# Token parts of 256 and 320 columns in layer 1, and 256-column halves in layer 2's second product

## The chip, the core and the metric

The kernel runs on one core of one Trainium2 chip. The metric is the device time of one execution in microseconds. The kernel before takes 853.9 us, the median of three runs (852.61 to 855.0).

## What is computed

The reference is a packed attention followed by two feed-forward layers, all in float32.

```python
# q, k, v: (4, 8, 576, 64); p: (4, 8, 32, 64)
p_packed = softmax(p @ k.T / 8) @ v          # 32 packed rows per head
x = softmax(q @ p_packed.T / 8) @ p_packed   # as (2304 tokens, 512)
h = x @ w1_in;  g = max(0.01 * h, h);  x = g @ w1_out      # 512 -> 2048 -> 512
h = x @ w2_in;  g = h * tanh(softplus(h));  out = g @ w2_out
```

2304 tokens are 4 batches of 576. The weights arrive as 64-bit floats and are converted on the chip.

## The kernel before, in words

Every large product is made of three matmuls on operands in the float32r type: each operand is split into a rounded part (index 0, "hi") and the rest (index 1, "lo"), and `PASSES` lists hi x hi, hi x lo, lo x hi. The first index picks the stationary operand (the weights that are loaded into the array), the second the moving one (whose columns stream through). So two of three passes in a row have the same stationary operand. Each such `mm` call gives one weight load (LDWEIGHTS) and one matmul in the trace; an `mm` on plain float32 operands gives two of each. The warm-up `warm` (L604 to L607) is of the second kind: 16 calls of 128 x 128 by 128 columns, called four times at the start, 128 matmuls in the trace.

Layer 1's first product (`l1_h`, L372 to L394) is folded with the attention: `packed_w` (L354 to L370) multiplies the packed values with `w1_in`, and `l1_h` multiplies the result `pw` (stationary, 128 x 128) with the attention weights `a2` (moving) of one batch. One call makes 128 of the 2048 hidden features for one half of a batch, `HALF` = 288 tokens, in 6 matmuls (2 head groups x 3 passes) into one PSUM bank `ps_h1` (tag "h", 2 buffers). ScalarE applies the leaky ReLU twice, rounded into `gx[:, 0]` and in full into `gf` (L391, L392), and VectorE writes the difference into `gx[:, 1]` (L393). `gf` has 3 buffers, `gx` 4; the tag "gx" is lent to attention tiles early on (`spare`, L199).

`l1_y` (L403 to L428) multiplies `w1_out` (stationary, four blocks `e` of 128 output features) with `gx` (moving, 288 columns): 12 matmuls that add into four banks `ps_y` (tag "y", 4 buffers, so all four belong to one part of the tokens at a time). At the last feature of a part the banks are evicted into `yp` blocks of `TB` = 384 tokens; a part that crosses a block's edge is evicted in two pieces (L422 copy on ScalarE, L424 add on VectorE). In the second pass `y_parts` splits finished blocks into `yh` and `yl` (L437, L439).

The order of this work is the list `slots` (L338 to L346): pass, batch, half `hb`, feature `f`; 128 slots, each one `l1_h` and, three slots later (`LAG`), one `l1_y`. Between the matmuls `tick` issues background steps (attention of later batches, `packed_w`, weight conversion) by a fixed plan, the string `SCHED`: a plan by counted ticks, not by time. The main loop waits, while the program is built, until the attention weights of the slot's half are there (L655). The whole program is issued in this written order; every engine runs its instructions in order.

Layer 2 goes through 96 steps of one feature block of 128 for one block of 384 tokens. `l2_h` (L444 to L455): 12 matmuls of 384 columns, `w2_in` stationary, `yh`/`yl` moving. `l2_g` (L457): two Mish activations and a subtraction. `l2_o` (L468 to L488), two steps later: the tokens are now the stationary operand (`gx`, three groups of 128) and `w2_out` the moving one, all 512 columns at once: 9 matmuls into three banks `ps_o`, evicted after each fourth step. The PE order is thus 12 matmuls of 384, 9 of 512, 12 of 384, and so on.

Of the kernel before, what the change touches and what calls it, by code (L numbers as in the profile page):

```python
# [8 lines left out]
F32 = mybir.dt.float32  # L9
F32R = mybir.dt.float32r  # L10
# [19 lines left out]
def tile_packed_attention_moe2(ctx: ExitStack, tc: tile.TileContext, q, k, v, p, w1i, w1o, w2i, w2o, out):  # L30
    nc = tc.nc
    B, H, S, D = q.shape
# [3 lines left out]
    R = 6  # L36
    SP = S // R
    HALF = S // 2
    NG = H // 4
    NE = DM // 128  # L40
    TB = 384
# [4 lines left out]
    mm = nc.tensor.matmul  # L46
# [5 lines left out]
    ident = const.tile([128, 128], F32, name="ident")  # L52
    ppT = const.tile([128, B * NG, 2, 2 * NP], F32, name="ppT")

    prog = {"h": -1, "y": -1, "pw": -1, "yb": -1, "h2": -1, "o": -1, "cv": -1}
# [6 lines left out]
    wi, wo, w2a, w2b = {}, {}, {}, {}  # L62
# [89 lines left out]
    a2_t = {}  # L152
    packed, ready = set(), set()
# [4 lines left out]
    def load_wide(src, nm, u):  # L158
        b, g = divmod(u, NG)
        if nm == "k":  # L160
            t = pwp.tile([SP, 4, R, D], F32, tag="pw", name=f"st_{nm}")
        else:
            t = ylp.tile([SP, 4, R, D], F32, tag="yl", name=f"st_{nm}")
        nc.sync.dma_start(t.rearrange("p h r d -> p h (r d)"), src[b, 4 * g : 4 * g + 4].rearrange("h (p r) d -> p h (r d)", r=R))
        staged[nm, u] = t
# [16 lines left out]
    def load_v(u):  # L182
        if u >= B * NG:
            return
        b, g = divmod(u, NG)
        t = ylp.tile([SP, 4, R, D], F32, tag="yl", name="raw_v") if u == 1 else raw.tile([SP, 4, R, D], F32, tag="rawv", name="raw_v")
        nc.sync.dma_start(t.rearrange("p h r d -> p h (r d)"), v[b, 4 * g : 4 * g + 4].rearrange("h (p r) d -> p h (r d)", r=R))
        raws["v", u] = t

    def load(src, nm, u):  # L190
        if u >= B * NG:
            return
        b, g = divmod(u, NG)
        t = raw.tile([SP, R, 4, D], F32, tag="raw" + nm, name=f"raw_{nm}")
        for h in range(4):
            nc.sync.dma_start(t[:, :, h, :], src[b, 4 * g + h].rearrange("(p r) d -> p r d", r=R))
        raws[nm, u] = t.rearrange("p r h d -> p r (h d)")

    def spare(nm):  # L199

        return gp.tile([128, S], F32, tag="gx", name=nm, bufs=4)

    def transpose_in(t, o, bank):
        for hp in range(2):
            for hb in range(2):
                ps = bank()
                for r in range(3):
                    nc.tensor.transpose(ps[:, r * SP : (r + 1) * SP], t[:, 3 * hb + r, 128 * hp : 128 * hp + 128], ident[:SP, :SP])  # L208
                nc.scalar.copy(o[hp][:, hb * HALF : (hb + 1) * HALF], ps[:, :HALF])
                yield  # L210

    def pack(u, bank, first=False):
# [12 lines left out]
        for hb in range(2):  # L225
            ps = bank()
            for hp in range(2):
                mm(ps[64 * hp : 64 * hp + 64, :HALF], pT[:, 2 * u + hp, :], kT[hp][:, hb * HALF : (hb + 1) * HALF], start=True, stop=True)  # L228
            nc.vector.reduce_max(mx2[:, hb : hb + 1], ps[:, :HALF], axis=AX.X)
            sc.append(ps)  # L230
# [6 lines left out]
        for hb in range(2):  # L237
            nc.scalar.activation(
                e1[:, hb * HALF : (hb + 1) * HALF], sc[hb][:, :HALF], AF.Exp, bias=nmb, scale=c_s, accum_out=sm2[:, hb : hb + 1]
            )  # L240
# [40 lines left out]
    def spread(u, bank, first=False):  # L281
# [11 lines left out]
        for hb in range(2):  # L293
            ps = bank()
            for hp in range(2):
                mm(ps[64 * hp : 64 * hp + 64, :HALF], ppT[:, u, hp, :], qT[hp][:, hb * HALF : (hb + 1) * HALF], start=True, stop=True)  # L296
            nc.vector.transpose(out=bt[:, hb * HALF : (hb + 1) * HALF], in_=ps[:, :HALF])
            yield
# [41 lines left out]
    for pas in range(2):  # L340
        for b in range(B):
            n_g = 2 if b in SPLIT[pas] else 1
            for c in range(n_g):
                for hb in range(2):
                    w = 8 // n_g
# [26 lines left out]
    def l1_h(i):  # L372
        pas, b, hb, f = slots[i][:4]
        pw = pw_t[(pas * B + b) * 2 + f % 8 // 4]
        fc = f % 4 * 128
        ps = psh.tile([128, 512], F32, tag="h", name="ps_h1")[:, :HALF]
        n = 0
        for g in range(NG):
            for x, y in PASSES:
                mm(  # L380
                    ps,
                    pw[:, g, x, fc : fc + 128],
                    a2_t[b, g][:, y, hb * HALF : (hb + 1) * HALF],
                    start=n == 0,
                    stop=n == 3 * NG - 1,
                )
                n += 1
        prog["h"] = i
        gf = gp.tile([128, HALF], F32, tag="gf", name="gf", bufs=3)
        gx = gp.tile([128, 2, HALF], F32R, tag="gx", name="gx", bufs=4)  # L390
        nc.scalar.activation(gx[:, 0], ps, AF.Prelu, alpha=0.01)  # L391
        nc.scalar.activation(gf, ps, AF.Prelu, alpha=0.01)  # L392
        nc.vector.tensor_tensor(out=gx[:, 1], in0=gf, in1=gx[:, 0], op=ALU.subtract)  # L393
        return gx  # L394
# [3 lines left out]
    def block(d, pool, dt, k, tag, nm):  # L398
        if k not in d:
            d[k] = pool.tile([128, NE, TB], dt, tag=tag, name=f"{nm}{k}")  # L400
        return d[k]

    def l1_y(i, gx, tick):  # L403
        pas, b, hb, f, first, last, part, final = slots[i]
        if first:
            ystate["b"] = [psy.tile([128, 512], F32, tag="y", name="ps_y") for _ in range(NE)]
        yb = ystate["b"]

        pieces, c = [], 0
        while c < HALF:  # L410
            k, o = divmod(b * S + hb * HALF + c, TB)
            n = min(TB - o, HALF - c)
            pieces.append((k, c, o, n))
            c += n
        for e in range(NE):
            for n, (x, y) in enumerate(PASSES):
                mm(yb[e][:, :HALF], wo[f][:, x, e * 128 : (e + 1) * 128], gx[:, y], start=first and n == 0, stop=last and n == 2)  # L417
            if last:
                for k, c, o, n in pieces:
                    dst = block(ypart, ylp, F32, k, "yl", "yp")[:, e, o : o + n]  # L420
                    if pas == 0 and part == 0:
                        nc.scalar.copy(dst, yb[e][:, c : c + n])  # L422
                    else:
                        nc.vector.tensor_tensor(out=dst, in0=yb[e][:, c : c + n], in1=dst, op=ALU.add)  # L424
            tick()
        prog["y"] = i
        if last and final and pas == 1:
            spawn(y_parts(pieces))  # L428
# [39 lines left out]
    def l2_o(s, gx, tick):  # L468
        fq, blk, fi = s // (4 * NB2), s // 4 % NB2, s % 4
        if fi == 0:  # L470
            ostate["b"] = [pso.tile([128, 512], F32, tag="o", name="ps_o") for _ in range(3)]
        ob = ostate["b"]
        w = w2b[fq * 4 + fi]
        if fq == 0 and fi == 3:
            outp[blk] = op_.tile([128, 3, 512], F32, tag="op", name="op")
        for t in range(3):
            for n, (x, y) in enumerate(PASSES):
                mm(ob[t], gx[:, x, t * 128 : (t + 1) * 128], w[:, y], start=fi == 0 and n == 0, stop=fi == 3 and n == 2)  # L478
            if fi == 3:
                dst = outp[blk][:, t]  # L480
                if fq == 0:
                    nc.scalar.copy(dst, ob[t])
                else:
                    nc.vector.tensor_tensor(out=dst, in0=ob[t], in1=dst, op=ALU.add)  # L484
                if fq == 3:
                    store(dst, blk * TB + t * 128)
            tick()
        prog["o"] = s  # L488
# [45 lines left out]
    def wait_for(cond):  # L534
        n = 0
        while not cond():
            tick(True)
            n += 1
            assert n < 1000

    with tc.manual_schedule():

        with ExitStack() as st1:
            a2p = st1.enter_context(tc.tile_pool(name="a2p", bufs=1, side="right"))
            pwp = st1.enter_context(tc.tile_pool(name="pwp", bufs=2, side="right"))
            gp = st1.enter_context(tc.tile_pool(name="gp", bufs=3, side="right"))
            psa = st1.enter_context(tc.tile_pool(name="psa", bufs=2, space=PSUM))
            psh = st1.enter_context(tc.tile_pool(name="psh", bufs=2, space=PSUM))
# [38 lines left out]
            for n in range(3, 8):  # L587
                x = ((n - 3) // 2 * NB2 + NB2 - 1) * 4 + (n - 3) % 2 * 2 + 1
# [59 lines left out]
            for i, (pas, b, hb, f, *_) in enumerate(slots):  # L648
                if pas and st_att is not None:
                    wait_for(lambda: (B * NG - 1, 1) in ready)  # L650
                    st_att.close()
                    st_att = None
                    yp = ctx.enter_context(tc.tile_pool(name="yp", bufs=1, reuse_waits="tile"))
                kk = (pas * B + b) * 2 + f % 8 // 4
                wait_for(lambda: prog["pw"] >= kk and all((b * NG + g, hb) in ready for g in range(NG)))  # L655
                pend.append((i, l1_h(i)))
                tick()
                if len(pend) > LAG:
                    i0, gx = pend.pop(0)
                    wait_for(lambda: slots[i0][3] in wo)  # L660
                    l1_y(i0, gx, tick)
# [49 lines left out]
```

## Time and profile before

| | |
|---|---|
| median of three runs | 853.9 us |
| the profiled execution's own time | 853.85 us |
| its span (first to last instruction) | 852.0 us |
| granted TensorE clock, mean | 0.997 |
| DMA, mean over the span | 63 GB/s |

The trace shows one execution. PE is TensorE's matmuls, PEld its weight loads, which overlap the matmuls; DVE is VectorE, ACT ScalarE, POOL GpSimd. Durations in the groups of instructions are those of one instruction in the pipe; neighbouring matmuls overlap, so the interval between two is read from the chain of waits or from their starts, not from the mean duration.

### The profile page before, as it was taken

To read this page: it belongs to the slowest core of one execution; us is meant where nothing else is said; L and a number is where in the kernel's file an instruction comes from. 1 tells how busy PE (TensorE), PEld (TensorE's weight loads), DVE (VectorE), ACT (ScalarE), POOL (GpSimd) and SP (SyncE) were. 2 spreads that over 40 slices of the span, in tenths; PEclk is the share of its full clock that TensorE was granted. 3 is DMA by queue.
4 is the path that set the end of the run, shared out by engine and by line. 5 is a ranking of instruction groups with operands and counts; after the bars stand their busy time and mean duration, and the time that the engine had idled before them with its cause. 6 is when DMAs were issued, how large, how long until landed. Compare 5 with 4: busy or idle time off the path is not lost.

```text
span 852.0 us, 13012 instructions
## 1 busy us (share of the span) xinstructions
PE 832.2 (98%) x5344; PEld 745.4 (87%) x5344; DVE 369.3 (43%) x725; ACT 308.5 (36%) x781; POOL 131.2 (15%) x134
## 2 busy tenths in 40 slices
PE   8889999999999999999999999999999999999997
PEld 7777789788999989898999999999999999999996
DVE  2787643533756733237574111342234532432222
ACT  3555445454444433434444223322223322222221
POOL 1233201101102211113343000120001200110000
PEclk9999999999999999999999999999999999999999
DMA  9963333220332300002132000230002200102112
GB/s 221 310 160 81 105 71 71 56 57 1 100 100 99 99 1 1 2 1 70 40 115 75 1 1 1 75 98 25 1 25 82 83 9 1 50 1 75 38 37 75
DMA packets 52570, 53.52 MB, mean 63 GB/s; under 512 B 31264, under 2 KB 44064, under 8 KB 52512
## 3 DMA queue, kind: packets, MB, share of 16 engines
q1 hardware_dynamic: 52512, 52.70, 21.9%
q8 instruction: 42, 0.69, 0.3%
q14 instruction: 16, 0.13, 0.1%
HBM read 47.97 MB, written 4.72 MB: 62 GB/s over the span
## 4 chain that ended last, share of the span: by engine, by line
PE 91%; DVE 4%; DMA 2%; ACT 1%; issue 1%; SPq 0%; POOL 0%; ACTq 0%; DVEq 0%; POOLq 0%
PE ps_h L452 24%; PE ps_o L478 23%; PE ps_y L417 23%; PE ps_h L380 11%; PE ps_pw L364 3%; DMA st_q<-in_q_dram 2%; PE ps_a L265 2%; PE ps_a L208 1%; PE ps_a L296 1%; PE ps_a L228 1%; PE ps_a L256 0%; DVE cv L129 0%; DVE cv L127 0%; DVE cv L131 0%; DVE gx L393 0%
## 5 line engine op out<-in xcount | busy, mean ns | idle before, releaser
L417 PE MATMUL ps_y<-gx,wo 128*128 128x288 f32 x1536 | 240.0, 300 | 1.1 <-DVE yp L424 1.1
L417 PEld LDWEIGHTS ps_y<-gx,wo 128*128 128x128 f32 x1536 | 212.6, 189 | 23.5 <-issue 15.8
L478 PE MATMUL ps_o<-w2b,gx 128*128 128x512 f32 x864 | 216.7, 395 | 0.0
L452 PE MATMUL ps_h<-yh,w2a 128*128 128x384 f32 x768 | 210.7, 335 | 0.0
L478 PEld LDWEIGHTS ps_o<-w2b,gx 128*128 128x128 f32 x864 | 161.6, 188 | 31.1
L463 DVE TENSOR_TENSOR gx<-gf,gx 128x384 fp32r<-128x384 f32 x96 | 54.2, 565 | 269.2 <-ACT gf L462 269.2
L461 ACT ACTIVATE gx<-ps_h 128x384 fp32r<-128x384 f32 x96 | 47.1, 491 | 269.3 <-PE ps_h L452 269.3
L452 PEld LDWEIGHTS ps_h<-yh,w2a 128*128 128x128 f32 x768 | 140.8, 188 | 3.8
L393 DVE TENSOR_TENSOR gx<-gf,gx 128x288 fp32r<-128x288 f32 x128 | 69.7, 544 | 144.9 <-ACT gf L392 144.2
L452 PE MATMUL ps_h<-yl,w2a 128*128 128x384 f32 x384 | 129.0, 336 | 0.0
L380 PE MATMUL ps_h<-a,pw 128*128 128x288 f32 x768 | 125.0, 297 | 2.4 <-ACT pw L365 1.8
L380 PEld LDWEIGHTS ps_h<-a,pw 128*128 128x128 f32 x768 | 108.5, 188 | 8.5 <-issue 3.8
L391 ACT ACTIVATE gx<-ps_h 128x288 fp32r<-128x288 f32 x128 | 52.6, 411 | 129.2 <-PE ps_h L380 129.1
L452 PEld LDWEIGHTS ps_h<-yl,w2a 128*128 128x128 f32 x384 | 72.0, 188 | 3.9
L140 POOL TENSOR_TENSOR w2a<-cv,w2a 128x512 fp32r<-128x512 f32 x16 | 21.9, 1370 | 226.4 <-ACT w2a L139 226.4
L392 ACT ACTIVATE gf<-ps_h 128x288 f32<-128x288 f32 x128 | 52.2, 408 | 0.0
L462 ACT ACTIVATE gf<-ps_h 128x384 f32<-128x384 f32 x96 | 46.5, 484 | 0.0
L439 POOL TENSOR_TENSOR yl<-yp,yh 128x288 fp32r<-128x288 f32 (+2 forms) x48 | 31.9, 690 | 83.3 <-ACT yh L437 82.9
L129 DVE SCALAR_TENSOR_TENSOR cv<-st,cv 128x512 uint32<-128x512 uint32 x48 | 40.1, 835 | 1.1
L140 POOL TENSOR_TENSOR wo<-cv,wo 128x512 fp32r<-128x512 f32 x16 | 20.9, 1304 | 108.2 <-ACT wo L139 108.2
L484 DVE TENSOR_TENSOR op<-ps_o,op 128x512 f32<-128x512 f32 x54 | 34.5, 683 | 3.5 <-PE ps_o L478 3.5
L131 DVE SCALAR_TENSOR_TENSOR cv<-st,cv 128x512 uint32<-128x512 uint32 x48 | 34.5, 719 | 1.0
(109 smaller groups left out, 565.6 us busy)
## 6 DMA issues: line engine op xcount, KB each, us to landing
st<-in_moe_w_in_dram SPq DMA_DIRECT2D x32, 512.0 KB, 3.8
st<-in_moe_w_out_dram SPq DMA_DIRECT2D x32, 512.0 KB, 3.5
raw_v<-in_v_dram SPq DMA_DIRECT2D x8, 576.0 KB, 4.8
raw_k<-in_k_dram SPq DMA_DIRECT2D x24, 144.0 KB, 3.3
raw_q<-in_q_dram SPq DMA_DIRECT2D x24, 144.0 KB, 3.1
out_dram<-op SPq DMA_DIRECT2D x12, 192.0 KB, 2.3
out_dram<-op SPq DMA_DIRECT2D x12, 128.0 KB, 2.4
st_k<-in_k_dram SPq DMA_DIRECT2D x2, 576.0 KB, 6.0
```

The costliest lines, as they stand in the source:

```text
L129: nc.vector.scalar_tensor_tensor(out=d, in0=hi, scalar=0xC0000000, in1=d, op0=ALU.bitwise_and, op1=ALU.bitwise_or)
L140: nc.gpsimd.tensor_tensor(out=t[:, j, 1], in0=x, in1=t[:, j, 0], op=ALU.subtract)
L380: mm(ps, pw[:, g, x, fc : fc + 128], a2_t[b, g][:, y, hb * HALF : (hb + 1) * HALF], start=n == 0, stop=n == 3 * NG - 1,)
L391: nc.scalar.activation(gx[:, 0], ps, AF.Prelu, alpha=0.01)
L392: nc.scalar.activation(gf, ps, AF.Prelu, alpha=0.01)
L393: nc.vector.tensor_tensor(out=gx[:, 1], in0=gf, in1=gx[:, 0], op=ALU.subtract)
L417: mm(yb[e][:, :HALF], wo[f][:, x, e * 128 : (e + 1) * 128], gx[:, y], start=first and n == 0, stop=last and n == 2)
L452: mm(ps, w[:, x, c, :], y2[y][:, c, :], start=n == 0, stop=n == 3 * NE - 1)
L461: nc.scalar.activation(gx[:, 0], ps, AF.Mish)
L462: nc.scalar.activation(gf, ps, AF.Mish)
L463: nc.vector.tensor_tensor(out=gx[:, 1], in0=gf, in1=gx[:, 0], op=ALU.subtract)
L478: mm(ob[t], gx[:, x, t * 128 : (t + 1) * 128], w[:, y], start=fi == 0 and n == 0, stop=fi == 3 and n == 2)
```

## The change

Layer 1's two parts of a batch become 256 and 320 tokens, tiles that hold a part are made 320 wide and cut to the part's width, and `gf` goes from 3 to 2 buffers. The wait for the attention weights asks, for the second part, for both 288-token halves. In layer 2's second product each matmul of 512 columns becomes two of 256 columns into the halves of the same bank, with the same stationary operand; only the first half's first matmul carries the start flag.

```diff
+    TW = 256
+    PARTS = ((0, TW), (TW, S - TW))
+    GW = S - TW
-        return gp.tile([128, S], F32, tag="gx", name=nm, bufs=4)
+        return gp.tile([128, 2 * GW], F32, tag="gx", name=nm, bufs=4)[:, :S]
...
-        ps = psh.tile([128, 512], F32, tag="h", name="ps_h1")[:, :HALF]
+        c0, W = PARTS[hb]
+        ps = psh.tile([128, 512], F32, tag="h", name="ps_h1")[:, :W]
-                    a2_t[b, g][:, y, hb * HALF : (hb + 1) * HALF],
+                    a2_t[b, g][:, y, c0 : c0 + W],
-        gf = gp.tile([128, HALF], F32, tag="gf", name="gf", bufs=3)
-        gx = gp.tile([128, 2, HALF], F32R, tag="gx", name="gx", bufs=4)
+        gf = gp.tile([128, GW], F32, tag="gf", name="gf", bufs=2)[:, :W]
+        gx = gp.tile([128, 2, GW], F32R, tag="gx", name="gx", bufs=4)[:, :, :W]
...
+        c0, W = PARTS[hb]
-        while c < HALF:
-            k, o = divmod(b * S + hb * HALF + c, TB)
-            n = min(TB - o, HALF - c)
+        while c < W:
+            k, o = divmod(b * S + c0 + c, TB)
+            n = min(TB - o, W - c)
-                mm(yb[e][:, :HALF], wo[f][:, x, e * 128 : (e + 1) * 128], gx[:, y], start=first and n == 0, stop=last and n == 2)
+                mm(yb[e][:, :W], wo[f][:, x, e * 128 : (e + 1) * 128], gx[:, y], start=first and n == 0, stop=last and n == 2)
...
-                mm(ob[t], gx[:, x, t * 128 : (t + 1) * 128], w[:, y], start=fi == 0 and n == 0, stop=fi == 3 and n == 2)
+                for j in range(2):
+                    mm(
+                        ob[t][:, j * 256 : (j + 1) * 256],
+                        gx[:, x, t * 128 : (t + 1) * 128],
+                        w[:, y, j * 256 : (j + 1) * 256],
+                        start=fi == 0 and n == 0 and j == 0,
+                        stop=fi == 3 and n == 2,
+                        skip_group_check=True,
+                    )
...
-                wait_for(lambda: prog["pw"] >= kk and all((b * NG + g, hb) in ready for g in range(NG)))
+                wait_for(lambda: prog["pw"] >= kk and all((b * NG + g, x) in ready for g in range(NG) for x in range(hb + 1)))
```

## Rows read from the trace of the kernel before

**Rows 1.** The page: busy time by engine, and two lines of the slices.
```profile
PE 832.2 (98%) x5344; PEld 745.4 (87%) x5344; DVE 369.3 (43%) x725; ACT 308.5 (36%) x781; POOL 131.2 (15%) x134
...
PE   8889999999999999999999999999999999999997
```

**Rows 2.** Stretches: length, busy us and instructions by engine, granted clock, DMA.
```profile
core 0: us, PE busy (x) PEld busy (x) DVE busy (x) ACT busy (x) POOL busy (x), PEclk, DMA share, GB/s
...
300.00:400.00 100.00, 100.00 (x704) 90.26 (x703) 37.39 (x77) 40.31 (x114) 21.12 (x30) 1.00 0.04 12
...
440.00:600.00 160.00, 160.00 (x817) 145.41 (x816) 50.25 (x86) 51.94 (x111) 23.90 (x23) 1.00 0.13 40
```

**Rows 3.** Waits of the matmul engine: total us, times, longest us.
```profile
PE ps_c L607 <- POOL ident masks.py:199: 3.1, 1, 3.1
PE ps_b L208 <- ACT e L238: 2.0, 1, 2.0
PE ps_h L380 <- ACT pw L365: 1.8, 1, 1.8
PE ps_c L208 <- ACT raw_q L173: 1.4, 1, 1.4
PE ps_a L208 <- ACT e L238: 1.2, 1, 1.2
PE ps_y L417 <- DVE yp L424: 1.1, 2, 0.7
```

**Rows 4.** Groups by line and shape: busy us, mean ns | idle before.
```profile
L417 PE MATMUL ps_y<-gx,wo 128*128 128x288 f32 x1536 | 240.0, 300 | 1.1 <-DVE yp L424 1.1
L478 PE MATMUL ps_o<-w2b,gx 128*128 128x512 f32 x864 | 216.7, 395 | 0.0
L417 PEld LDWEIGHTS ps_y<-gx,wo 128*128 128x128 f32 x1536 | 212.6, 189 | 23.5 <-issue 15.8 <-DVE yp L424 1.6 <-DVE pw L366 1.6
L452 PE MATMUL ps_h<-yh,w2a 128*128 128x384 f32 x768 | 210.7, 335 | 0.0
L478 PEld LDWEIGHTS ps_o<-w2b,gx 128*128 128x128 f32 x864 | 161.6, 188 | 31.1
...
L452 PE MATMUL ps_h<-yl,w2a 128*128 128x384 f32 x384 | 129.0, 336 | 0.0
L380 PE MATMUL ps_h<-a,pw 128*128 128x288 f32 x768 | 125.0, 297 | 2.4 <-ACT pw L365 1.8 <-POOL a L330 0.6
```

**Rows 5.** Chain of waits in layer 2: start us, us, what.
```profile
449.86 2.10 PE ps_o L478 x9
451.95 2.09 PE ps_h L452 x12
454.05 2.10 PE ps_o L478 x9
456.15 2.10 PE ps_h L452 x12
```

**Rows 6.** The same chain in layer 1.
```profile
300.33 0.79 PE ps_h L380 x6
301.13 1.60 PE ps_y L417 x12
302.73 0.79 PE ps_h L380 x6
303.52 1.60 PE ps_y L417 x12
```

**Rows 7.** Groups of ScalarE and VectorE in layer 1, by shape.
```profile
L393 DVE TENSOR_TENSOR gx<-gf,gx 128x288 fp32r<-128x288 f32 x128 | 69.7, 544 | 144.9 <-ACT gf L392 144.2
L391 ACT ACTIVATE gx<-ps_h 128x288 fp32r<-128x288 f32 x128 | 52.6, 411 | 129.2 <-PE ps_h L380 129.1
L392 ACT ACTIVATE gf<-ps_h 128x288 f32<-128x288 f32 x128 | 52.2, 408 | 0.0
...
L424 DVE TENSOR_TENSOR yp<-ps_y,yp 128x288 f32<-128x288 f32 x28 | 11.1, 449 | 0.7 <-PE ps_y L417 0.6
...
L424 DVE TENSOR_TENSOR yp<-ps_y,yp 128x192 f32<-128x192 f32 x28 | 9.7, 346 | 0.0
...
L424 DVE TENSOR_TENSOR yp<-ps_y,yp 128x96 f32<-128x96 f32 x28 | 6.9, 246 | 0.0
```

**Rows 8.** Waits of VectorE: total us, times, longest us.
```profile
DVE gx L393 <- ACT gf L392: 144.2, 102, 3.1
```

**Rows 9.** Timeline of PE in the start: first start us, us to last end.
```profile
39.82 3.07 PE L607 MATMUL ps_c<-ident 128*128 128x128 f32 x26
```

**Rows 10.** Groups of the warm-up matmuls, by shape.
```profile
L607 PE MATMUL ps_c<-ident 128*128 128x128 f32 x128 | 16.8, 294 | 3.1 <-POOL ident masks.py:199 3.1
L607 PEld LDWEIGHTS ps_c<-ident 128*128 128x128 f32 x128 | 16.2, 209 | 3.5 <-POOL ident masks.py:199 3.1 <-issue 0.4
```

## The prediction

> **What bounds the kernel now.** I read the page's busy shares first: the matmul engine is busy 832.2 of 852.0 us, its weight loads 745.4, every other engine 43% or less, and its slices show it at nine tenths or more from the fourth slice to the last but one [rows 1]. Next the table by stretches: between 300 and 400 us and between 440 and 600 us the matmul engine is busy for the whole stretch at a granted clock of 1.00, which is the 2.4 GHz level [rows 2]. Then the list of waits: what the matmul engine waits for is first work of the start (identity, first transposes, first packed weights) and a rest of single waits of 1.2 us or less, some 14 us in all [rows 3]. So the time is the sum of the intervals between matmuls, and only an edit that changes this sum counts. The groups of instructions give the counts: 1536 and 768 matmuls of 288 columns (layer 1), 1152 of 384 columns and 864 of 512 (layer 2) [rows 4]. Their mean durations (300, 335, 395 ns) are no intervals, since matmuls overlap in the pipe; intervals come from the chain of waits, which counts each matmul from the end of the one before.
>
> **The interval of one matmul.** The chain's pieces in layer 2 [rows 5]: 12 matmuls of 384 take 2.09 to 2.10 us, 9 of 512 take 2.10 us. Both are 4608 columns. Three matmuls and three weight loads more cost nothing that this view can tell; the time goes by columns, 2.10/4608 = 0.456 ns each, 233 ns for 512 columns, 175 for 384. In layer 1 [rows 6] one slot is 6 + 12 matmuls of 288: 0.79 + 1.60 = 2.39 us for 5184 columns, 132.8 ns each. With a cost c for each matmul and s for each column, 9c + 4608s = 2.10 and 18c + 5184s = 2.39 give c = 3.5 ns; the two layer-2 pieces give c = 0. These are the two ends for what one more matmul costs.
>
> **Part 1: layer 1 in 256 and 320 columns.** Nothing is removed or added: still 128 slots of 18 matmuls, 64 of them now 256 wide and 64 now 320. The widths of two slots sum to 576 as before, and c and s both cancel: 64 x (18 x 256s + 18 x 320s) equals 128 x 18 x 288s. ACT's two activations and DVE's subtraction are also linear in width, 411, 408 and 544 ns at 288 [rows 7], so a pair of slots costs them the same; in the narrow slot they need about 0.73 us of ACT and 0.5 of DVE against 2.1 us of matmuls, so they stay covered. The evictions of the y banks are cut at the 384-token blocks: pieces of 288, 96 + 192, 192 + 96, 288 become 256, 128 + 192, 192 + 64, 320, the same number over the same columns, on rows where 288, 192 and 96 take 449, 346 and 246 ns [rows 7]. The longest line of pieces at one part's end is 128 + 192 in place of 96 + 192, some 30 ns more on each of four banks; the existing waits on that eviction are 1.1 us in two [rows 3], so I allow 0.3 us. The buffers of gf go from three to two: ACT may not write slot i + 2 before DVE has subtracted slot i, two slots or 4.2 to 4.8 us later. DVE stood waiting for gf 102 times over its 128 subtractions [rows 7, 8], so it follows within a slot; cost nothing, and if that cover were gone ACT would hold a ps_h bank and the matmul engine would stop. The new condition (part 1 needs both 288-token halves of a2) only adds halves that were already waited for when part 0 of the same batch began. The one place where the unequal slots matter is the stretch before 230 us, where the background work (transposes, packing) is laid into ticks by count and not by time: narrow slots give it 11% less cover, wide ones give it back. The single waits there are about a us each [rows 3]; I allow -1 to +2 us, and take 0.
>
> **Part 2: the second product in halves.** 864 matmuls of 512 become 1728 of 256, and 864 weight loads become 1728: matmuls that follow each other with the same weights already load them each time, as the equal counts of loads and matmuls show (1536 and 1536 in L417, where two of three passes share weights) [rows 4]. No DMA, ACT or DVE instruction is added; the eviction waits for the last half as it did for the last matmul. In one group of 9 the columns stay 4608, so it goes from 2.10 to 2.10 + 9c: with c = 0 nothing, with c = 3.5 ns 31.5 ns. Over 96 groups: 0 to +3.0 us. The place speaks for the lower end (the 0 was read at this very product), the width for the upper (288 is nearest to 256); I take the middle, +1.5 us. This stands on the second weight load being hidden. The rows nearest to a load at that pace are the warm-up matmuls of 128 columns in full float32, each with a 128 x 128 load: 26 in 3.07 us [rows 9], less one duration of 0.29 [rows 10], over 25 intervals is 111 ns. That is below 256 x 0.456 = 117 ns, by 6 ns only.
>
> By the Trainium skill (TensorE: Matmul & The Clock Gate, section Back-to-back issue gap) a warm matmul takes its columns over 2.4 GHz plus 2.5 ns; the trace departs: 216 ns by the page for 512 columns against the 233 above. Its fixed 2.5 ns would make part 2 cost 864 x 2.5 = 2.2 us.
>
> **The sum.** The profiled execution took 853.85 us, span 852.0 and 1.85 around it; the median of the three runs is 853.9, the same within 0.1. 853.9 + 0 (part 1) + 1.5 (part 2) = 855.4 us.
>
> **Rivals.**
> *A. Weight loads become the bound (slower).* Place: all 256-wide matmuls, 1728 in layer 2 and 64 x 18 = 1152 in layer 1. The 111 ns was seen beside matmuls of 128 columns, which read their columns at 0.87 ns each, half the pace of 0.456; beside a stream at full pace the load may be slower. From below it is bounded by that 111, from above by the 132.8 at which load and stream fit today. It decides from 117 ns on. At 120 ns: 96 x (18 x 0.120 - 2.10) = +5.8 us in layer 2, and 1152 x (120 - 132.8 x 256/288 = 118) ns = +2.3 in layer 1: 862 us. At 132.8 it would be 96 x 0.29 = 27.8 and 1152 x 14.8 ns = 17, 899 us. For it: a load's record lasts 188 ns [rows 4], longer than 117. Against it: the warm-up loads have records as long (209 ns in the mean) [rows 10] and still follow each other at 111.
> *B. 256 columns escape the excess (faster).* At 2.4 GHz 512 columns are 213 ns; they take 233, 384 take 175 instead of 160, 288 take 133 instead of 120: 9% more than the clock asks for. If that excess belongs to streams longer than 256 columns, a 256-wide matmul falls to the pace of its weight load, 111 ns: layer 2 96 x (2.10 - 18 x 0.111) = -9.8 us, layer 1 1152 x (118 - 111) ns = -8.1: 836 us; at half the effect 845. Against it: the excess over three widths is proportional to the columns (20, 15, 13 ns) and does not shrink towards 288. For it: no row has a float32r stream of 256, and the cause of the excess is not in the profile.
> The Trainium skill's section named above would have it so too: by its formula 256 columns take 109 ns. The trace does not agree with it at any of the three widths.
> *C. Part 1 disturbs the early stage.* Waits before 230 us grow by more than the 2 us allowed, because DVE's evictions come late to a narrow part. About 858. Most early waits are of data that no slot width moves.
>
> **How the numbers follow.** Forecast (no change that counts): 0.54; own range 852.5 to 859 (part 1's -1 to +2.3, part 2's 0 to +3). A 0.18, B 0.25, C 0.03. About 0.3%, 2.6 us, is what a measurement of this kernel can tell from no change. The forecast's chance divides into 0.37 within it, 0.05 faster and 0.12 slower, since +1.5 lies nearer the upper edge. Faster: 0.25 + 0.05 = 0.30. Slower: 0.18 + 0.03 + 0.12 = 0.33. Same: 0.37. The range goes down to B's full price, 836, and up to 861, which leaves out most of A: about 0.17 outside.
>
> **What will show it.** In the chain after, a group of 18 matmuls of 256 beside 12 of 384: 2.10 to 2.13 us is the forecast, 2.16 or more is A, 2.0 is B. In layer 1 a narrow slot of about 2.12 us and a wide one of 2.65, sum 4.78: the sum tells part 1 from part 2. The count of loads in the second product must be 1728, or the halves share a load and A falls away. The list of waits of the matmul engine should keep its entries, none new above 1 us; a wait of ACT's gf on DVE would show the two buffers too few. The forecast is wrong if 256 columns have a pace of their own, on either side of 117 ns.

## The result and the profile after

The changed kernel takes 858.27 us (median of 4 runs, 857.18 to 859.23) against 853.77 for the kernel before (4 runs on the same chip). The ratio is 1.0052, its 95% interval 1.0033 to 1.0071: 2.8 to 6.1 us slower. The profiled execution took 857.18 us, its span 855.4, 3.4 us over the span before.

The page's busy line (first fence) answers to [rows 1], the table by stretches (second fence, columns as in [rows 2]) shows one stretch of layer 2, before and then after: the matmul engine is full at a granted clock of 1.00 in both, the 2.4 GHz level.

```profile
PE 835.0 (98%) x6208; PEld 786.0 (92%) x6208; DVE 369.5 (43%) x725; ACT 307.8 (36%) x781; POOL 130.5 (15%) x134
```

```profile
460.00:820.00 360.00, 360.00 (x1805) 325.28 (x1804) 114.28 (x197) 96.18 (x211) 28.56 (x21) 1.00 0.12 36
460.00:820.00 360.00, 360.00 (x2572) 360.00 (x2571) 113.75 (x196) 96.30 (x211) 29.43 (x22) 1.00 0.12 37
```

864 matmuls and as many weight loads have come in. In layer 2 the records of the loads now fill the stretch too, 360.00 of 360.00 us where it was 325.28; the next rows show that this costs little. The chain of waits in layer 2 answers to [rows 5]:

```profile
451.83 2.12 PE ps_o L486 x18
453.95 2.09 PE ps_h L458 x12
456.04 2.12 PE ps_o L486 x18
458.16 2.09 PE ps_h L458 x12
```

9 matmuls of 512 took 2.10 us, 18 of 256 take 2.12 (2.113 between the starts of the groups). 96 groups x 13 ns are 1.3 us. In layer 1 the same chain answers to [rows 6]; first a wide output product beside a narrow first product, then two narrow slots:

```profile
315.76 0.72 PE ps_h L385 x6
316.48 1.77 PE ps_y L423 x12
...
325.05 0.71 PE ps_h L385 x6
325.75 1.44 PE ps_y L423 x12
327.19 0.71 PE ps_h L385 x6
327.90 1.43 PE ps_y L423 x12
...
331.49 0.88 PE ps_h L385 x6
```

(The piece of 1.77 is the output product of a wide slot, 0.88 at 331.49 the first product of one; each output product comes three slots after its first product, so 0.72 and 1.77 stand side by side.) A narrow slot takes 2.15 us, a wide one 2.64 to 2.65, the two about 20 ns more than two slots of 2.39. Last the waits of the matmul engine (total us, times, longest), of which [rows 3] lacks the second:

```profile
PE ps_y L423 <- DVE yp L430: 1.2, 2, 0.9
...
PE ps_y L423 <- POOL wo L144: 0.9, 1, 0.9
```

The timelines of PE and POOL around it, after the change:

```profile
292.49 0.44 PE L423 MATMUL ps_y<-gx,wo 128*128 128x256 f32 x2
293.78 1.46 PE L423 MATMUL ps_y<-gx,wo 128*128 128x256 f32 x10 [0.85 <-POOL wo L144]
...
292.45 1.27 POOL L144 TENSOR_TENSOR wo<-cv,wo 128x512 fp32r<-128x512 f32 x1 [2.29 <-ACT wo L143]
```

and before it:

```profile
293.78 1.76 PE L417 MATMUL ps_y<-gx,wo 128*128 128x288 f32 x12
...
292.56 1.28 POOL L140 TENSOR_TENSOR wo<-cv,wo 128x512 fp32r<-128x512 f32 x1 [2.25 <-ACT wo L139]
```

These are the matmuls of the same slot (the eighth of the second pass) and the conversion of its weights. The conversion ends at the same time, 293.72 and 293.84 us. The matmuls come at 292.49 instead of 293.78, for seven narrow output products in a row have gone before; the third matmul needs the low part of the weights and stands. Before, the third matmul came at about 294.05, 0.2 us after the conversion.

**Where the time went.** The table below takes two stretches of each trace by the starts of matmuls: from the first matmul of slot 16 to the first of layer 2, and from there to the last matmul's end. The runs from e1 on are described in the next section.

| | slot 16 to layer 2, us | layer 2, us |
|---|---|---|
| before | 334.73 | 402.71 |
| after | 337.36 | 403.99 |
| e1_layer1_only | 337.48 | 402.74 |
| e2_layer2_only / e12 (same program) | 334.69 / 334.68 | 403.99 / 403.99 |
| e3_layout_only / e13 (same program) | 333.82 / 333.85 | 402.74 / 402.74 |
| e5_wide_first | 336.42 | 402.70 |
| e11_parts_272_304 | 334.54 | 402.72 |

Layer 2 costs 1.28 us. Layer 1 costs 2.63 in its stretch, of which 0.5 is no cost: slot 16 begins with three wide output products still to come from slots 13 to 15, each 0.167 longer than at 288 columns (1.765 and 1.598 between starts). The rest, 2.1, is the wait of 0.9 and 56 pairs x 20 ns = 1.1. With the 8 pairs before slot 16 (0.16) and 0.1 behind the last matmul the traces account for 3.6 us, which lies within the 2.8 to 6.1 of the timed runs. The stretch ahead of slot 16 can't be used to the tenth of a us, as the repeated program below shows.

### The profile page after: what moved, and what is told of

Its sections match the earlier page's. It is cut to its first block, busy times and chain, and to the rows that moved or that the text cites. A ratio compares the mean times of both kernels' runs of the same rounds, so it can differ in the third digit from the quotient of the medians.

```text
span 855.4 us, 14741 instructions
## 1 busy us (share of the span) xinstructions
PE 835.0 (98%) x6208; PEld 786.0 (92%) x6208; DVE 369.5 (43%) x725; ACT 307.8 (36%) x781; POOL 130.5 (15%) x134
## 4 chain that ended last, share of the span: by engine, by line
PE 89%; DVE 4%; DMA 2%; issue 1%; ACT 1%; POOL 1%; SPq 0%; POOLq 0%; ACTq 0%; DVEq 0%
PE ps_o L486 24%; PE ps_h L458 23%; PE ps_y L423 22%; PE ps_h L385 11%; PE ps_pw L368 3%; DMA st<-in_moe_w_in_dram 2%; PE ps_a L269 2%; PE ps_a L212 1%; PE ps_a L300 1%; PE ps_a L232 1%; DVE cv L135 0%; PE ps_a L260 0%; DMA raw_q<-in_q_dram 0%; DVE cv L133 0%; DVE cv L131 0%
## 5 line engine op out<-in xcount | busy, mean ns | idle before, releaser
L423 PE MATMUL ps_y<-gx,wo 128*128 128x320 f32 (+1 forms) x1536 | 240.4, 300 | 2.1 <-DVE yp L430 1.2
L486 PE MATMUL ps_o<-w2b,gx 128*128 128x256 f32 x1728 | 218.4, 280 | 0.0
L486 PEld LDWEIGHTS ps_o<-w2b,gx 128*128 128x128 f32 x1728 | 215.0, 188 | 0.0
L398 DVE TENSOR_TENSOR gx<-gf,gx 128x256 fp32r<-128x256 f32 (+1 forms) x128 | 69.1, 541 | 147.9 <-ACT gf L397 147.8
L385 PE MATMUL ps_h<-a,pw 128*128 128x256 f32 (+1 forms) x768 | 126.5, 300 | 2.8 <-ACT pw L369 2.1
L396 ACT ACTIVATE gx<-ps_h 128x256 fp32r<-128x256 f32 (+1 forms) x128 | 52.7, 412 | 130.1 <-PE ps_h L385 129.9
L397 ACT ACTIVATE gf<-ps_h 128x256 f32<-128x256 f32 (+1 forms) x128 | 52.2, 407 | 0.0
L445 POOL TENSOR_TENSOR yl<-yp,yh 128x192 fp32r<-128x192 f32 (+4 forms) x48 | 31.3, 679 | 84.5 <-ACT yh L443 84.2
```

The lines of the kernel that those rows point to most:

```text
L385: mm(ps, pw[:, g, x, fc : fc + 128], a2_t[b, g][:, y, c0 : c0 + W], start=n == 0, stop=n == 3 * NG - 1,)
L423: mm(yb[e][:, :W], wo[f][:, x, e * 128 : (e + 1) * 128], gx[:, y], start=first and n == 0, stop=last and n == 2)
L486: mm(ob[t][:, j * 256 : (j + 1) * 256], gx[:, x, t * 128 : (t + 1) * 128], w[:, y, j * 256 : (j + 1) * 256], start=fi == 0 and n == 0 and ...
```

## The experiments

**Each part alone.** e1 is the changed kernel with the second product back at 512 columns, e2 the kernel before with it in halves:

```diff
-                for j in range(2):        # e1: one matmul of 512 again
-                    mm(ob[t][:, j * 256 : (j + 1) * 256], ..., w[:, y, j * 256 : (j + 1) * 256], ...)
+                mm(ob[t], gx[:, x, t * 128 : (t + 1) * 128], w[:, y], start=fi == 0 and n == 0, stop=fi == 3 and n == 2)
```

> Only layer 1's parts are changed (256 and 320 columns, wider tiles, two gf buffers); layer 2's second product keeps its 512-column matmuls. My theory before the result (a small fixed cost for each matmul): the number of layer-1 matmuls is unchanged, so no difference, within 0.1% of the kernel before. The trace of the changed kernel says otherwise: six plus twelve matmuls take 721 + 1436 ns at 256 columns and 884 + 1765 at 320, sum 4806, against 2 x (795 + 1598) = 4786 at 288; 20 ns x 64 pairs = 1.3 us slower, and up to 2 us with the early waits. If 256 columns are bound by their weight load (rival A), the 256 slots alone are long, 120 ns per matmul where the columns ask for 116 to 117: about +3 us.

> Only layer 2's second product is changed (two matmuls of 256 columns for one of 512); layer 1 as before. Small fixed cost for each matmul: a group goes from 2.100 to about 2.113 us (the changed kernel's trace), 96 x 13 ns = 1.3 us slower, no wait anywhere else. If the whole change of 4.5 us lies here, by something outside the groups (instruction fetch, the tail), the time is 858 and the chain shows it.

e1: ratio 1.0042 (1.0030 to 1.0054). Layer 1's stretch is long by 2.75 us, as in the changed kernel, and the same wait stands in the list:

```profile
PE ps_y L423 <- DVE yp L430: 1.3, 2, 0.9
PE ps_y L423 <- POOL wo L144: 0.8, 1, 0.8
```

So the 1.3 us expected from the trace was right and not all: the wait comes to it, and its 0.9 us had not been reckoned. e2: ratio 1.0028 (1.0017 to 1.0039), in the trace 1.28 us and nothing elsewhere. The two timed ratios add up to 0.70%, more than the 0.52% of both changes together, and e2's lies above its trace. I ran e2's program again:

> The same program as e2_layer2_only, to tell its 1.3 us of the trace (96 groups of 2.113 in place of 2.100 us) from its 2.4 us of the timed runs (0.17% to 0.39%). If the trace has the whole cost, the ratio is 1.0015 (+1.3 us). If something outside the groups costs about 1 us more (the start, where the clock's half-speed stretches fall differently), it is 1.0025 to 1.003 again.

Ratio 1.0003 (0.9994 to 1.0012). The same program was 2.4 us slower in one set of runs and 0.3 in the next, while both traces give the same 334.7 and 403.99 us. What differs is the start. The first 60 us of the two traces, by stretches (columns as in [rows 2]), e2 and then its repetition:

```profile
0.00:60.00 60.00, 51.70 (x430) 44.49 (x431) 35.65 (x83) 29.47 (x70) 17.93 (x24) 0.91 0.89 238
```

```profile
0.00:60.00 60.00, 52.56 (x451) 45.40 (x452) 38.28 (x88) 30.98 (x74) 17.94 (x24) 0.97 0.90 245
```

The clock granted in the first 60 us was 0.91 in the first and 0.97 in the second. In both the matmul engine waited 1.8 us for the first packed weights, until 48.17 and 46.08 us; from 48 to 53 us the clock stood at 0.66 in the mean in e2, part of it at the 1.2 GHz level, and at 1.00 in the repetition. Slot 16 starts at 109.77 and 107.04 us. The clock is not the whole of it: up to slot 16 the kernel before is the same program, its clock there was 0.97 too, and its slot 16 starts at 108.72 us. From 60 us on the clock is 1.00 in all three. The intervals of the timed ratios do not cover what such starts do from one set of runs to the next; the stretches behind the start are free of it, and by them 1.3 us is what the halves cost.

**Layout without the widths.** The wider tiles and two gf buffers, but parts of 288 and 288:

```diff
-    PARTS = ((0, TW), (TW, S - TW))
+    PARTS = ((0, HALF), (HALF, HALF))
```

> The changed kernel's layer-1 tiles (320 wide, two gf buffers, cut to the part's width) but with parts of 288 and 288 as before, and 512-column matmuls in layer 2. If the layer-1 cost lies in the widths: no difference from the kernel before. If it lies in the layout (rows of gx 1280 bytes apart) or the missing gf buffer: the same 1.3 to 2 us slower as with the parts of 256 and 320.

> The same program as e3_layout_only, as the candidate for a version faster than both kernels: by its trace a pair of slots takes 4.760 in place of 4.786 us, 64 pairs, and layer 1 from slot 16 on is 0.9 us shorter. If that is all, the ratio is 0.999 (-0.9 us), an interval that may reach 1; if the first look was chance, it is at or over 1.

Ratios 0.9994 (0.9986 to 1.0003) for e3 and 0.9995 (0.9984 to 1.0005) for e13. So neither the lost buffer nor the wider rows cost anything: the price of layer 1 is the widths'. The layout even gives a little, 0.9 us in layer 1's stretch both times, in the chain

```profile
326.18 0.79 PE ps_h L385 x6
326.97 1.59 PE ps_y L423 x12
328.56 0.79 PE ps_h L385 x6
329.35 1.58 PE ps_y L423 x12
```

2.375 us a slot here against 2.39. It is faster than the changed kernel, but timing does not tell it from the kernel before. Which part of the layout gives it (rows of `gx` 1280 bytes apart in place of 1152, the buffers) was not tried.

**What a weight load needs.** The kernel before with 512 columns cut into 320 and 192:

```diff
-                mm(ob[t], gx[:, x, t * 128 : (t + 1) * 128], w[:, y], ...)
+                for c0, c1 in ((0, 320), (320, 512)):
+                    mm(ob[t][:, c0:c1], gx[:, x, t * 128 : (t + 1) * 128], w[:, y, c0:c1], ...)
```

> Layer 2's second product in matmuls of 320 and 192 columns in place of 256 and 256; layer 1 as before. It shows what a weight load needs beside a full-pace stream. Small fixed cost for each matmul and loads hidden: 192 columns take about 88 to 90 ns and 320 about 145 to 147, a group of 18 again 2.11 us. Load at the pace of the warm-up matmuls: 192 columns take 111 ns, a group 9 x (111 + 146) = 2.31 us, +20 us in all. Load-bound already at 256 (rival A): 192 columns take the same 117 ns as 256 did, a group 2.37 us, +26 us.

877.15 us, beside 854.2. The chain of it:

```profile
601.53 2.30 PE ps_o L479 x18
603.83 2.13 PE ps_h L452 x12
```

A group takes 2.30 us: the middle expectation, 111 ns for the narrow matmul. Less nine matmuls of 320 at 147 ns, nine of 192 take (2.30 - 1.32)/9 = 109 ns, where their columns ask for 88. The starts of the loads in this trace say the same: the load that starts beside a narrow matmul is followed by the next after 108 to 110 ns all through layer 2. (The starts of the matmuls hide it: 88 ns from a narrow one to the next, some 168 from a wide one.) So a 128 x 128 float32r load paces at 109 ns beside a full stream too, near the 111 of the warm-up matmuls [rows 9]. 192 columns are bound by it, 256 in layer 2 (117 ns) are not. The Trainium skill (TensorE: Matmul & The Clock Gate, section LDWEIGHTS) puts a load's ns at its columns over 1.2; an estimate by it for 128 columns is 107. The pace in the traces agrees within 4 ns; a load's record, 188 ns [rows 4], is longer.

**The wait for the converted weights.** e1 with the wide part first in the second pass:

```diff
-    PARTS = ((0, TW), (TW, S - TW))
+    PARTS = (((0, TW), (TW, S - TW)), ((0, S - TW), (S - TW, TW)))
...
-        c0, W = PARTS[hb]
+        c0, W = PARTS[pas][hb]
...
```

> Layer 1 alone in parts of 256 and 320 (as in e1_layer1_only), but in the second pass the wide part comes first: 320, then 256. In the changed kernel the matmul engine waits 0.9 us at 293 us for a converted block of the layer-1 output weights, right after eight narrow slots in a row. If narrow slots overtake the conversion, that wait is gone and layer 1 is about 0.9 us shorter than in e1_layer1_only (2.7 - 0.9 = 1.8 us longer than before from slot 16 to layer 2). If the wait has another cause (place in the order, the conversion late by itself), it stays within 0.3 us.

The list of waits from slot 16 on has no POOL wo left:

```profile
PE ps_y L423 <- DVE yp L430: 1.2, 3, 0.5
PE ps_h L385 <- POOL a L334: 0.7, 1, 0.7
```

and layer 1's stretch is 336.42 us, 1.06 shorter than e1's and 1.69 longer than before; 0.9 and 1.8 were expected. So the wait came from narrow slots that run ahead of the conversion.

**Why 256 columns take 120 ns in layer 1 and 117.4 in layer 2.** Three ideas, three runs: neighbours that add onto the same columns (e6, layer 2 with the halves outside the passes), two banks in turn (e7, the output product in pairs of e), the rows of gx close together (e8).

```diff
# e6, on the kernel before, with the halves
-            for n, (x, y) in enumerate(PASSES):
-                for j in range(2):
+            for j in range(2):
+                for n, (x, y) in enumerate(PASSES):
# e7, on e1
-        for e in range(NE):
-            for n, (x, y) in enumerate(PASSES):
+        for e0 in range(0, NE, 2):
+            for n, (x, y) in enumerate(PASSES):
+                for e in (e0, e0 + 1):
...
# e8, on e1
-        gx = gp.tile([128, 2, GW], ...)[:, :, :W]
+        gx = gp.tile([128, 2 * GW], ...)[:, : 2 * W].rearrange("p (y w) -> p y w", y=2)
```

> Layer 2's second product in halves of 256 columns, but all three passes of one half before the other, so that neighbouring matmuls add into the same 256 columns; layer 1 as before. Theory 1 (256 columns cost more where a matmul adds onto the columns its neighbour has just written): 120 ns each as in layer 1's narrow slots, a group of 18 at 2.16 us. Theory 2 (layer 1's narrow slots are dear for a reason of layer 1): 117.4 ns as with alternating halves, 2.113 us.

> Layer 1 alone in parts of 256 and 320, with the twelve matmuls of the output product reordered so that neighbours add into two different banks in turn. Theory 1 (adding onto the columns just written is what makes 256 dear): the twelve take 12 x 117.4 = 1.41 us in place of 1.436 in a narrow slot, the six of the first product stay at 0.721. Theory 2: 1.436 as before.

> Layer 1 alone in parts of 256 and 320; the two rows of gx of a narrow part lie 1024 bytes apart and not 1280. Theory 3 (the spacing of the moving operand's rows sets the excess): the twelve matmuls of a narrow slot differ from 1.436 us by more than 10 ns, and the first product (which does not read gx) stays at 0.721. Otherwise 1.436, within 3 ns.

The chain of each in turn, e6, e7 and e8:

```profile
602.68 2.12 PE ps_o L479 x18
```

```profile
327.18 0.71 PE ps_h L385 x6
327.89 1.43 PE ps_y L425 x12
```

```profile
328.62 1.43 PE ps_y L423 x12
330.06 0.71 PE ps_h L385 x6
```

Nothing moves: 2.12 us with neighbours on the same columns, 1.43 to 1.44 with banks in turn and with close rows. All three ideas fall. The reason for the 2 to 3 ns stays open. That loads take part in it, since they need 109 of the 120 ns, is not excluded; against it stands layer 2, where as many loads of the same size leave 117.4, also in e6, which repeats a stationary operand in the same order as layer 1.

e7's time, 858.76 us, has another cause. The banks of a pair are given up later, and near the end of layer 1 the matmul engine waits 1.7 us on one eviction; the timeline of PE, and the stretches around it (columns as in [rows 2]):

```profile
439.38 9.06 PE L425 MATMUL ps_y<-gx,wo 128*128 128x320 f32 x48 [1.71 <-DVE yp L436]
```

```profile
400.00:438.00 38.00, 37.44 (x274) 36.34 (x272) 24.15 (x52) 15.13 (x43) 11.06 (x13) 1.00 0.21 70
438.00:446.00 8.00, 6.62 (x33) 6.45 (x34) 5.84 (x14) 3.85 (x13) 6.30 (x10) 0.79 0.32 98
```

From 438 to 446 us, which begins in that pause, the clock is granted at 0.79 in the mean, part of it at the 1.2 GHz level. e1 waits 1.3 us on the same evictions, in two pieces of which the longer is 0.9, and its clock in the same stretch is 1.00. Layer 1's stretch is 340.18 us, 2.7 over e1's, and 2.0 of it lie behind the start of the last slot: there 0.4 us more of waiting cost 2.0. The other 0.7 us, before it, were not traced.

**Two more widths.** e1 with `TW = 272`:

> Layer 1 alone in parts of 272 and 304 columns. With 256, 288 (same tiles) and 320 known at 120, 132.2 and 147.2 ns, two more widths tell whether 256 is a case by itself. A curve that goes by columns: 272 takes 125 to 126 ns, 304 139 to 140, and a pair of slots stays near 2 x 2.380 us. If narrowing itself costs (each step away from the middle): 272 takes 126 to 127 and 304 140, a pair 10 to 30 ns over 4.760 us. The wait for the converted output weights (0.9 us with 256) shrinks or goes, since eight slots of 272 take 0.7 us longer.

```profile
301.78 0.83 PE ps_h L385 x6
302.61 1.68 PE ps_y L423 x12
...
325.78 0.75 PE ps_h L385 x6
326.53 1.51 PE ps_y L423 x12
```

853.18 us in the one run, beside 854.75; one run of each doesn't tell them apart. With the pieces of this chain (1.50 to 1.51 and 1.67 to 1.68), of e3 and of the changed kernel, the twelve matmuls of an output product give for one matmul 119.7 ns at 256 columns, 125.5 at 272, 132 at 288, 139.5 at 304, 147 at 320. The steps of 16 columns are 6, 6.5, 7.5, 7.5 ns: the curve bends. The six matmuls of a first product, by their starts in the same traces, bend at another place: 119.7, 125.5, 131.8, 138.0, 147.2 ns. Over both products the pair of 272 and 304 takes some 5 to 14 ns more than two slots of 288 in the same layout, the pair of 256 and 320 some 46. So the cost of unequal parts grows with their distance in the two cases tried, and little of it comes at the first step. The wait for the converted weights is 0.3 us here, as expected less than 0.9.

**Where the 9% over one column per clock at 2.4 GHz belongs.** The kernel before with the second product's operands in bfloat16 (less exact), two token groups in 512 columns and the third in halves:

```diff
-        gx = gp2.tile([128, 2, TB], F32R, tag="gx", name="gx2", bufs=4)
+        gx = gp2.tile([128, 2, TB], BF16, tag="gx", name="gx2", bufs=4)
...
-                mm(ob[t], gx[:, x, t * 128 : (t + 1) * 128], w[:, y], ...)
+                for c0, c1 in ((0, 512),) if t < 2 else ((0, 256), (256, 512)):
+                    mm(ob[t][:, c0:c1], gx[:, x, t * 128 : (t + 1) * 128], w[:, y, c0:c1], ...)
```

> Layer 2's second product on bfloat16 operands (both gx and the second weights are rounded to bfloat16 pairs, so the output is less exact), the first two token groups with 512 columns per matmul, the third in halves of 256; everything else as before. If the 9% above 2.4 GHz belongs to the float32r stream: 512 columns take 213 to 216 ns in place of 233, 256 take 107 to 111. If it belongs to the place (banks, neighbours, memory traffic): 233 and 117 as in float32r. The difference between two halves and one whole is the fixed cost of a matmul without the load's limit: 1 to 3 ns by the skill's and by the float32r reading (13 ns over 9).

839.71 us beside 854.75. The group of 6 + 6 matmuls, over the same 4608 columns, in the chain:

```profile
601.06 2.09 PE ps_h L453 x12
603.15 1.97 PE ps_o L480 x12
```

2.10 has become 1.97 us; neighbouring starts lie 216 ns apart at 512 columns and 109 at 256. The excess goes with the operand type and not with the place. Whether it belongs to the columns or to the loads beside them the run does not tell, for the loads became bfloat16 too: their records last 98 ns in place of 188. By the formula that the Trainium skill (TensorE: Matmul & The Clock Gate, section Back-to-back issue gap) gives for a matmul by itself an estimate is 216 and 109 ns: the trace agrees for bfloat16, and for float32r it does not (233 and 117). Two halves less one whole are 2 x 109 - 216 = 2 ns in bfloat16, 13/9 = 1.5 in float32r.

## Why the prediction was right or wrong

**The range and the side.** 858.27 lies in the range, on the slower side. The likeliest case, no change beyond 2.6 us, was not what came: 4.5 us in the timed runs, 3.6 accounted for in the traces. That the time still lies within 852.5 to 859 is luck in part: the allowance of part 1 was made for waits before 230 us, and what used it up came from elsewhere.

**Part 2, the halves: right.** 0 to 3.0 us with 1.5 taken; 1.28 measured, 1.5 ns for each matmul more. That the second load is hidden at 256 columns is shown by e2 and e4. That the 1.5 ns are a fixed cost of each matmul is argued: a pace that depends on the width, as in layer 1, would look the same. And the 1.5 us was the middle of two readings, neither of which was a cost of one matmul: by starts instead of rounded pieces (2.093 and 2.100 us in layer 2, 2.393 in layer 1) they are -2 and +4 ns. That their middle came close to 1.28 us is luck.

**Part 1, the widths: the step that failed** is "c and s both cancel". The interval in layer 1 is not a straight line in the columns: it bends between 256 and 320 (e11), so that 18 x (119.7 + 147) ns are more than 36 x 132.8. Why it bends stays open. By the prediction's own sign, "a pace of their own, on either side of 117 ns", the forecast is wrong in layer 1 (119.7) and holds in layer 2 (117.4); a narrow and a wide slot were to sum to 4.78 us and take 4.806. The term of 0 should have been 20 ns x 64 = 1.3 us; against the same layout with equal parts (e3) it is 46 ns, by 4.806 and 4.760 us a pair between starts. The rows could have warned: with c from layer 1 and c from layer 2 three and a half ns apart, the line through three widths was no line, and the 13 ns of excess at 288 columns are 11% of 120, not the 9% of the wider ones. I spread this over part 2 and let part 1 cancel.

**The cover of the background work: right in kind, wrong in place.** The prediction looked for trouble "before 230 us", where the ticks are dense; the engine's waits there sum to 12.8 us before and 12.3 after. Trouble came at 293 us, in a stretch without waits before the change, where the conversion of weights had 0.2 us of slack that no list of waits shows. Its 0.9 us are of the size that was allowed (-1 to +2), but not in the 0 that was taken.

**Costed at nothing, and rightly:** two gf buffers (e3; the changed kernel's list of waits has none of ACT on DVE for gf either), the evictions (1.2 us of waits in place of 1.1), the new condition on a2 (the longest wait for it is 0.7 us in place of 0.6).

**Rival A** (loads become the bound) falls at 256 columns: the pace of a load is 109 to 111 ns, and 256 columns take 117 to 120. In layer 1 the 119.7 ns lie close to the 120 that A was priced at, but layer 2, with the same loads, stays at 117.4. A would have come true at 192 (e4, +23 us). **Rival B** (256 columns escape the excess) falls: layer 2's halves keep the 9%; float32r shows the excess at every width measured. **Rival C** (waits before 230 us, by late evictions) did not come: the wait above is a later one and has another cause.

## What to carry to other kernels

Splitting a matmul into two with the same stationary operand doubled the loads here (1728 in place of 864). At 256 columns the split cost about 1.5 ns a matmul in layer 2; at 192 the load, 109 to 111 ns, set the pace. An estimate of where the one turns into the other, from 111 ns and 0.456 ns a column, is 243 columns. In layer 1 parts of equal width beat unequal ones though the columns sum to the same, first because the interval bends with the width and second because a run of narrow parts overtakes background work that was laid out by count: look for the producer that ends just ahead of its reader, since a slack of 0.2 us stands in no list of waits. When an effect is a few us in 850, compare the same stretch of two traces rather than whole times.

## What the runs showed of the hardware

- A float32r stream takes 0.454 ns a column (12 of 384 in 2.09 us) to 0.468 (119.7 ns at 256, layer 1) at a granted clock of 1.00, the 2.4 GHz level; bfloat16 at the same place takes 216 ns for 512, 0.42 a column (e9).
- A 128 x 128 load in float32 or float32r is followed by the next after 108 to 112 ns where loads are the bound (e4, and the warm-up matmuls of [rows 9]), though its record lasts 188 to 209 ns.
- The stretches of one program agree between two executions within 0.03 us over some 334 us and 0.00 over 403 (e2 and e12, e3 and e13), while the time to slot 16 differs by 2.7 us (e2 and e12), with a granted clock of 0.91 and 0.97 in the first 60.
- 256 columns of float32r take 117.4 ns with the tokens as stationary operand and 119.7 to 120 in layer 1; neighbours on the same columns, banks in turn and row spacing don't explain it.
